# Gated attention mix on one core: a maxima product takes the PSUM bank whose last read stands first in VectorE's order, instead of a fixed turn of four

## The chip, the cores and the metric

The kernel runs on one core of a Trainium2 chip. The metric is the device time of one execution in microseconds (us); the number compared is the median of several runs. A profile is one execution taken by the hardware profiler; its span runs from the first to the last instruction.

The engines are named as the profile names them: PE is TensorE (PEld are its weight loads), DVE is VectorE, ACT is ScalarE, POOL is GpSimd, SP issues most DMAs. Each works through its own instructions in a fixed order and waits on semaphores for the others. Matmul results go to PSUM, which has eight banks of 128 x 512 float32 numbers here called by their tiles' names.

## What is computed

The input x has 2048 rows of 512 numbers. Two attentions of 32 heads of 16 numbers are formed on it and mixed by a gate:

```
q, k, v = x @ wqkv                                   # attention A, over all 2048 keys
o = softmax(q k^T * 0.25) v;  a = o @ wo
# attention B, in 4 segments of 512 rows, masked inside the segment:
p = softmax(q_s k_s^T * 0.25 + mask);  a_dot = p v_s
o = sig(beta) * a_mem + (1 - sig(beta)) * a_dot      # a_mem: memory of the earlier segments
b = o @ wo
g = sigmoid(sum(x * gate_w));  out = g * a + (1 - g) * b
```

Each softmax needs the largest score of each row before the exponentials, so that these cannot overflow.

## The kernel before

**Two stages.** In the first stage (up to about 300 us) the projections are computed and stored in DRAM. In the second, the work is cut into 64 units, 32 of side A and 32 of side B: a unit is four heads and one segment of 512 queries. A unit of A has 64 slots, a unit of B 10 slots, 2368 slots in all, and the second stage is one loop over slots, `n`.

**What one slot does.** `score_part(n)` (scores L744) multiplies keys by queries into a bank of the pool `st`, three banks in turn, and ScalarE takes the exponential into `p` (L767). `max_part(m)` works 96 slots ahead, `m = n + LEAD`: it forms scores of a later unit the other way round, queries by keys, in one of four fixed banks `sm0` to `sm3` (L205, called a maxima product here), and VectorE reduces the bank to row maxima. These are later put as extra rows beside that unit's queries, so that the score product subtracts them itself. After every third slot (`BURST` = 3) come the value products of older units, `ops` += v p (L801), or projections and output products that fill in. So TensorE's order in a burst is score, maxima, score, maxima, score, maxima, then values. The order of every engine is written out by the program; nothing is scheduled at run time.

**How VectorE reads a bank.** A product of side A fills a whole bank and is read by one TENSOR_REDUCE (L226). A product of side B has one or two pieces in the same bank, each read by a masked reduction (L238, in the profile CUSTOM_DVE_ANT_0 with a short DVE_READ_ACCUMULATOR2_ANT behind it). Only the first piece is read at once; the second goes into the list `rows_left` and is read after the next product's own reduction (`flush_rows`). So a two-piece B product m is read in the order: first piece of m, product m+1, second piece of m, product m+2. A unit of B has ten products, six of them in two pieces: 192 in all.

**Which bank.** In the second stage the call is

```python
            max_part(m, lambda: banks[m % 4])
```

Product m+4 writes where product m was, and waits until VectorE's last read of product m is done. In the first stage, where the first 96 products are made, another pool is used (`me_sm`), which the change leaves alone.

**The end.** The last maxima product is made at slot n = 2271. From slot 2274 on (`wide`) every other burst of scores goes to `sm1`, `sm2`, `sm3` by a fixed turn, and output products to `sm0` (L913).

Of the kernel before, what the change touches and what calls it, by code (L numbers as in the profile page):

```python
# [13 lines left out]
ALU = mybir.AluOpType  # L14
# [8 lines left out]
CH = 512  # L23
# [24 lines left out]
def gated_mix(ctx, tc, x, xT, wqkv, a_wo, b_wq, b_wk, b_wv, b_wo, beta, gate_w, out):  # L48
    nc = tc.nc
# [60 lines left out]
    nS = len(slots)  # L110
# [64 lines left out]
    tri = {}  # L175
# [3 lines left out]
    def finish_max(u):  # L179
        nm = pmt.pop(u)  # L180
        if u[0] == "A":
            pm, nm = nm, mp.tile([128, 4, 4], F32, tag="nm", name="nm")
            nc.vector.tensor_reduce(nm, pm, axis=AX.X, op=ALU.max, negate=True)  # L183

        ms = mp.tile([128, 2, 2, 2, 4], F32R, tag="ms", name="ms")
        nv = nm.rearrange("p (r h) s -> p r h s", r=2)
        nc.gpsimd.tensor_copy(ms[:, :, 0], nv)  # L187
        nc.gpsimd.tensor_sub(ms[:, :, 1], nv, ms[:, :, 0].bitcast(F32))
        return ms
# [14 lines left out]
    def max_product(ps, u, h, s, n0, n, k, k0=0):  # L204
        nc.tensor.matmul(ps[:, n0:n0 + n], rows(qt[u][:, :, s * 128:(s + 1) * 128], h, 48), rows(k[:, :, k0:k0 + n], h, 48),  # L205
                         start=True, stop=True)

    rows_left = []

    def flush_rows():  # L210
        while rows_left:
            rows_left.pop(0)()

    def max_part(m, bank):

        u, (r, i) = maxs[m]
        side, g, c = u
        if u not in pmt:
            pmt[u] = mp.tile([128, 4, 4] + [4] * (side == "A"), F32, tag="pm" + side, name="pm")
        pm = pmt[u]  # L220
        ps = bank()
        if side == "A":

            kc, s, h = i // 8, i % 8 // 2, 2 * r + i % 2
            max_product(ps, u, h, s, 0, CH, kt_[u, kc])
            nc.vector.tensor_reduce(pm[:, h, s, kc:kc + 1], ps, axis=AX.X, op=ALU.max)  # L226
            flush_rows()
        else:


            k = kt_[u, c]
            mine = [(2 * r + h, s, 128 * (s == 2) + 256 * (s == 1 and h), 128 * (s + 1))
                    for h, s in (((0, 0), (0, 2)), ((0, 1), (1, 1)), ((1, 0), (1, 2)), ((0, 3),), ((1, 3),))[i]]
            for h, s, n0, w in mine:
                max_product(ps, u, h, s, n0, w, k)
            flush_rows()
            for h, s, n0, w in mine:
                rows_left.append(lambda h=h, s=s, n0=n0, w=w: nc.vector.tensor_tensor_reduce(  # L238
                    out=tri["rest"][:, 0:w], in0=ps[:, n0:n0 + w], in1=tri["mask"][:, CH - w:], scale=-1.0, scalar=3.0e38,
                    op0=ALU.add, op1=ALU.min, accum_out=pm[:, h, s:s + 1]))  # L240
            rows_left.pop(0)()
        if m == last_max[u]:
            def finish():

                due = min(e for e in a_last if e >= last_max[u]) + LATE_T
                late.append((min(due, first[u] + LEAD - 12), u, finish_max(u)))
            todo.append((m + 1, finish))

    def run_todo(m):

        for e in [e for e in todo if e[0] <= m]:
            todo.remove(e)
            e[1]()

    def run_late(pool, tag, m):
        while us := [e for e in late if e[0] < m][:2]:
            for e in us:
                late.remove(e)
            transpose_max(us, pool, tag)
# [3 lines left out]
    def loads(m):  # L263

        m = min(m, len(maxs) - 1)
        while loaded[0] <= m:
            u, (r, i) = maxs[loaded[0]]
            if loaded[0] == first_max[u]:
                load_q(u)
            kc = u[2] if u[0] == "B" else i // 8  # L270
            if (u, kc) not in kt_:
                load_k(u, kc)
            loaded[0] += 1
# [3 lines left out]
    with ExitStack() as p0:  # L277
# [282 lines left out]
        def some_max():  # L560
            m = mnext[0]
            if m == LEAD:
                return
            loads(m + 3 + PRE)
            for i in range(4):
                max_part(m + i, lambda: me_sm.tile([128, CH], F32, tag="sm", name="sm"))
            run_todo(m + 3)
            mnext[0] += 4
            run_late(me_ps, "me", mnext[0])
# [54 lines left out]
    banks = [sm_ps.tile([128, CH], F32, name=f"sm{i}") for i in range(4)]  # L624
# [383 lines left out]
    def most():  # L1008

        if not queue:  # L1010
            return 0
        side = queue[0][1][0]
        left = SLOTS[side] - queue[0][2]
        over = 64 * (len(queue) - LOW) > (HIGH - LOW) * (left if side == "A" else 0)
        return ends[side].get(left, MOST + over)
# [3 lines left out]
    while n < nS or queue or beside or filled[0] < len(fill):  # L1019
        for f in beside.pop(n, []):  # L1020
            f()
        if n < nS:
            score_part(n)
        m = n + LEAD
        if m < nS:
            loads(m + PRE)

            max_part(m, lambda: banks[m % 4])
        run_todo(m)
        if n >= nS or n % (2 * BURST if n in wide else BURST) == (2 * BURST if n in wide else BURST) - 1:  # L1030
            taken = 0
            if shared:
                for _ in range(3):
                    shared.pop(0)()
            else:
                taken = some_values(n, 8 if n >= nS or n in wide else most())
            if n < 5:


                for i in range(4):  # L1040
                    nc.tensor.matmul(ops[:, 128 * i:128 * i + 128], identf, identf, start=True, stop=True)
            if any(e[0] < m + 1 for e in late):
                run_late(st_ps, "st", m + 1)
            else:

                for _ in range(0 if n >= nS and queue else 4 if n not in wide else 11 - taken if taken < 8 else 0):
                    if filled[0] == len(fill) or fill[filled[0]][0] > n:
                        break
                    fill[filled[0]][1]()
                    filled[0] += 1  # L1050
        n += 1
# [12 lines left out]
def build():  # L1064
    import concourse.bacc as bacc
    nc = bacc.Bacc("TRN2", target_bir_lowering=False, num_devices=1)
    shapes = {"x": (S, D), "xT": (D, S), "wqkv": (D, 3 * D), "a_wo": (D, D), "b_wq": (D, D), "b_wk": (D, D),
              "b_wv": (D, D), "b_wo": (D, D), "beta": (H,), "gate_w": (D,)}
    args = [nc.dram_tensor(n, s, F32, kind="ExternalInput").ap() for n, s in shapes.items()]
    out = nc.dram_tensor("out", (S, D), F32, kind="ExternalOutput").ap()  # L1070
    with tile.TileContext(nc) as tc:
        gated_mix(tc, *args, out)
    return nc
# [23 lines left out]
```

## Time and profile before

| | |
|---|---|
| median of 3 runs | 1779.55 us (1779.37 to 1779.65) |
| the profiled execution's own time | 1779.57 us |
| its span | 1777.8 us |
| POOL busy | 641.2 us |
| ACT, exponentials L767, x2261 | 1189.5 us busy, 601 ns each |
| DVE, reductions L226, x2048 | 1281.1 us busy, 683 ns each |
| DVE, masked reductions L238, x512 | 247.3 us busy, 483 ns each |
| PE, maxima products of A, L205, x2048 | 660.4 us busy, 428 ns each |
| PE, maxima products of B, L205, x512 | 166.2 us busy, 385 ns each |

An instruction's duration is longer than the time it takes up: two reductions in a row overlap by some 0.08 us at their ends, and matmuls overlap much more, so counts times durations come to more than the busy time. "Idle before" is the time in which an engine did nothing ahead of an instruction, with the instruction whose semaphore ended it. An engine can start late by less than the overlap and show no idle time.

### The profile page before, as it was taken

The numbers are of one execution on the slowest core, as the hardware profiler recorded it, in microseconds if no ns is written. First come the engines' busy times: TensorE is split into PE (matmuls) and PEld (weight loads), VectorE is DVE, ScalarE is ACT, GpSimd is POOL, SyncE is SP. The second block draws the span as 40 slices with busy tenths as digits, with TensorE's granted clock in tenths as the row PEclk, the third lists the DMA queues.
The fourth block names the chain that finished last, engine by engine and source line by source line (L and its number), as shares of the span: only waits on it lengthen the run. The fifth ranks groups of instructions, "written<-read, shape, count | busy, mean of one in ns | idle before, by whom it ended". The sixth has DMA issues, their size and how long they took to land.

```text
span 1777.8 us, 40673 instructions
## 1 busy us (share of the span) xinstructions
PE 1770.5 (100%) x14945; PEld 915.2 (51%) x14945; DVE 1573.5 (89%) x3331; ACT 1435.4 (81%) x2752; POOL 641.2 (36%) x748
## 2 busy tenths in 40 slices
PE   9999999999999999999999999999999999999999
PEld 8887776444444444444444444444444444444444
DVE  4236777999999999999999999999999999999931
ACT  5455445888888888888888888888888888888884
POOL 3002223415161417443434343344434253435343
PEclk9999999999999999999999999999999999999999
DMA  7667566445453536555454544454545353544542
GB/s 251 212 234 239 182 205 187 121 110 134 128 152 107 147 108 179 143 146 128 132 143 121 145 127 146 128 146 126 147 112 154 113 141 116 150 119 138 144 160 62
DMA packets 141270, 261.55 MB, mean 147 GB/s; under 512 B 36328, under 2 KB 58888, under 8 KB 140560
## 3 DMA queue, kind: packets, MB, share of 16 engines
q1 hardware_dynamic: 139712, 257.55, 50.3%
q8 instruction: 119, 1.95, 0.5%
q0 software_dynamic: 1216, 1.14, 0.3%
q14 instruction: 79, 0.65, 0.1%
q10 hardware_dynamic: 144, 0.26, 0.0%
HBM read 174.39 MB, written 83.25 MB: 145 GB/s over the span
## 4 chain that ended last, share of the span: by engine, by line
PE 95%; DVE 1%; ACT 1%; DMA 1%; POOL 1%; issue 0%; SPq 0%; POOLq 0%; DVEq 0%
PE ops L801 33%; PE st L744 27%; PE sm L205 14%; PE pr L311 10%; PE ops L913 4%; PE ops L684 2%; PE sm L913 2%; PE num L514 1%; POOL mn L378 1%; PE pr L401 1%; PE mps L545 0%; DVE pm L226 0%; DMA qdB<-q 0%; PE mt_ps L196 0%; DMA raw<-xT 0%; PE sm L744 0%
## 5 line engine op out<-in xcount | busy, mean ns | idle before, releaser
L767 ACT ACTIVATE p<-st 128x512 f32<-128x512 f32 x2261 | 1189.5, 601 | 152.3 <-PE sm L205 108.2
L226 DVE TENSOR_REDUCE pm<-sm 128x1 f32<-128x512 f32 x2048 | 1281.1, 683 | 11.5 <-PE sm L205 11.3
L744 PE MATMUL st<-qA,kA 50*128 50x512 f32 x2014 | 663.4, 432 | 0.0
L205 PE MATMUL sm<-kA,qA 48*128 48x512 f32 x2048 | 660.4, 428 | 0.4
L801 PE MATMUL ops<-p,vA 128*17 128x128 f32 (+3 forms) x6432 | 552.0, 442 | 0.0
L744 PEld LDWEIGHTS st<-qA,kA 50*128 50x128 f32 x2014 | 328.0, 185 | 415.1 <-ACT p L767 370.6
L205 PEld LDWEIGHTS sm<-kA,qA 48*128 48x128 f32 x2048 | 331.7, 185 | 16.9 <-issue 4.6
L863 POOL TENSOR_TENSOR rcp<-rec,minus 128x32 f32<-128x32 f32 x43 | 234.2, 5446 | 76.4 <-DMA rec<-dend 71.8
L238 DVE CUSTOM_DVE_ANT_0 rest<-sm,mask 128x128 f32<-128x128 f32 (+3 forms) x512 | 247.3, 483 | 1.4
L801 PEld LDWEIGHTS ops<-p,vA 128*17 128x17 f32 x6432 | 130.5, 96 | 214.4 <-issue 189.4
L748 POOL TENSOR_SCALAR_AFFINE_SELECT p<-p 128x512 f32<-128x512 f32 x128 | 79.4, 636 | 324.9 <-ACT p L767 320.4
L205 PE MATMUL sm<-kB,qB 48*128 48x128 f32 (+3 forms) x512 | 166.2, 385 | 0.0
L744 PE MATMUL st<-qB,kB 50*128 50x512 f32 (+1 forms) x495 | 109.3, 330 | 0.3 <-ACT mt L199 0.3
L381 DVE TENSOR_TENSOR q<-full,q 128x512 fp32r<-128x512 f32 x56 | 38.6, 689 | 74.9 <-ACT q L374 67.9
L744 PEld LDWEIGHTS st<-qB,kB 50*128 50x128 f32 x495 | 69.9, 186 | 59.3 <-ACT p L767 48.6
L801 PE MATMUL ops<-p,vB 128*17 128x128 f32 (+3 forms) x1504 | 87.5, 350 | 0.0
L205 PEld LDWEIGHTS sm<-kB,qB 48*128 48x128 f32 x512 | 80.0, 184 | 0.0
L187 POOL CAST ms<-nm 128x16 fp32r<-128x16 f32 x32 | 6.3, 196 | 201.5 <-DVE nm L183 199.6
L378 POOL TENSOR_SCALAR mn<-full 128x512 f32<-128x512 f32 x24 | 36.4, 1515 | 102.5 <-ACT full L373 82.2
L373 ACT COPY full<-pr 128x512 f32<-128x512 f32 x56 | 32.8, 586 | 40.2 <-PE pr L311 37.3
L187 POOL CAST ms<-pm 128x16 fp32r<-128x16 f32 x32 | 6.3, 196 | 127.9 <-DVE pm L238 127.8
L801 PEld LDWEIGHTS ops<-p,vB 128*17 128x17 f32 x1504 | 33.1, 97 | 31.1 <-issue 26.6
(198 smaller groups left out, 1622.7 us busy)
## 6 DMA issues: line engine op xcount, KB each, us to landing
kA<-kdA SPq DMA_DIRECT2D x256, 128.0 KB
vA<-vdA SPq DMA_DIRECT2D x31, 544.0 KB
kA<-kdA SPq DMA_DIRECT2D x256, 64.0 KB
kdA<-q SPq DMA_DIRECT2D x32, 256.0 KB
qdB<-q SPq DMA_DIRECT2D x32, 256.0 KB
qA<-qdA SPq DMA_DIRECT2D x64, 128.0 KB
kdB<-q SPq DMA_DIRECT2D x32, 256.0 KB
qB<-qdB SPq DMA_DIRECT2D x64, 128.0 KB
```

What stands on the lines that cost most here:

```text
L205: nc.tensor.matmul(ps[:, n0:n0 + n], rows(qt[u][:, :, s * 128:(s + 1) * 128], h, 48), rows(k[:, :, k0:k0 + n], h, 48), start=True, stop=True)
L226: nc.vector.tensor_reduce(pm[:, h, s, kc:kc + 1], ps, axis=AX.X, op=ALU.max)
L238: rows_left.append(lambda h=h, s=s, n0=n0, w=w: nc.vector.tensor_tensor_reduce(out=tri["rest"][:, 0:w], in0=ps[:, n0:n0 + w], in1=tri["mas ...
L311: nc.tensor.matmul(ps, l(a, k), r(b, k), start=(n == 0), stop=(n == 11))
L378: nc.gpsimd.tensor_scalar_min(ph["mn"], full, 0.0)
L381: nc.vector.tensor_sub(q2, full, q1.bitcast(F32))
L744: nc.tensor.matmul(ps[:, n0:n0 + CH - q0], rows(k[:, :, b * 128:(b + 1) * 128], h, 50), rows(q[:, :, q0:], h, 50), start=True, stop=True)
L748: nc.gpsimd.affine_select(out=x, in_=x, pattern=[[0, 4], [1, 128]], base=0, channel_multiplier=-1, compare_op=ALU.is_ge, fill=0.0)
L767: nc.scalar.activation(p[:, h], ps, AF.Exp, scale=SCALE)
L801: nc.tensor.matmul(ops[32 * h:32 * h + 17, q0:q0 + 128 * w], v[:, 17 * h:17 * h + 17], p[:, h, c0:c0 + 128 * w], start=(i == 0), stop=done ...
L863: eng.tensor_tensor(r, rec, minus, op=ALU.pow)
L913: yield lambda i=i, x=x, w=w: nc.tensor.matmul(ps, t[:, b, x], halved[side][:, o, w], start=start and i == 0, stop=stop and i == 2)
```

## The change

The program now keeps, for each of the four banks, the place in VectorE's order of the bank's last read (`read_last`), and gives each maxima product of the second stage the bank with the earliest such place. The count goes up by one with each reduction that is issued. No instruction is added on VectorE or TensorE, and none changes its place: only the bank that each one names changes, and with it the semaphore value that a product waits for.

```diff
+    read_last = dict(zip(range(4), range(4)))
+
+    def oldest():
+
+        return min(read_last, key=read_last.get)
+
+    def was_read(b):
+
+        if b is not None:
+            read_last[b] = count[0] = count[0] + 1
+    count = [4]
+
-    def max_part(m, bank):
+    def max_part(m, bank, b=None):
...
             nc.vector.tensor_reduce(pm[:, h, s, kc:kc + 1], ps, axis=AX.X, op=ALU.max)
+            was_read(b)
             flush_rows()
         else:
...
             k = kt_[u, c]
+            if b is not None:
+                read_last[b] = 9 * nS
...
+            def masked(h, s, n0, w):
+                nc.vector.tensor_tensor_reduce(
+                    out=tri["rest"][:, 0:w], in0=ps[:, n0:n0 + w], in1=tri["mask"][:, CH - w:], scale=-1.0, scalar=3.0e38,
+                    op0=ALU.add, op1=ALU.min, accum_out=pm[:, h, s:s + 1])
+                was_read(b)
+
             for h, s, n0, w in mine:
-                rows_left.append(lambda h=h, s=s, n0=n0, w=w: nc.vector.tensor_tensor_reduce(
-                    out=tri["rest"][:, 0:w], in0=ps[:, n0:n0 + w], in1=tri["mask"][:, CH - w:], scale=-1.0, scalar=3.0e38,
-                    op0=ALU.add, op1=ALU.min, accum_out=pm[:, h, s:s + 1]))
+                rows_left.append(lambda h=h, s=s, n0=n0, w=w: masked(h, s, n0, w))
             rows_left.pop(0)()
...
-            max_part(m, lambda: banks[m % 4])
+            b = oldest()
+            max_part(m, lambda: banks[b], b)
```

The change adds lines, so that L226 of the kernel before is L238 now, L238 is L253, L744 is L763, L801 is L820; L205 keeps its number.

VectorE, around products 307 to 311 (at about 433 us of the profile). `ISA rest` is a masked reduction, the short `ISA pm` belongs to it; `sm0` to `sm3` are the banks (the number behind the underscore is the tile's own). Before:

```order
L226 TENSOR_REDUCE pm_4661<-sm3_3011 128x1
L238 ISA rest_3023,pm_4743<-sm2_3010,mask_3024 128x256
L238 ISA pm_4743 128x1
L226 TENSOR_REDUCE pm_4661<-sm0_3008 128x1
L238 ISA rest_3023,pm_4743<-sm1_3009,mask_3024 128x256
L238 ISA pm_4743 128x1
L226 TENSOR_REDUCE pm_4661<-sm2_3010 128x1
```

The rows are: product 307, second piece of 306, product 308, first piece of 309, product 310. Product 310 reads from `sm2`, the bank of 306, whose second piece was read after product 307.

The same rows now:

```order
L238 TENSOR_REDUCE pm_4661<-sm0_3008 128x1
L253 ISA rest_3023,pm_4743<-sm3_3011,mask_3024 128x256
L253 ISA pm_4743 128x1
L238 TENSOR_REDUCE pm_4661<-sm2_3010 128x1
L253 ISA rest_3023,pm_4743<-sm1_3009,mask_3024 128x256
L253 ISA pm_4743 128x1
L238 TENSOR_REDUCE pm_4661<-sm0_3008 128x1
```

Product 310 now reads from `sm0`, the bank of 307, whose only read stands one place earlier than the second piece of 306.

TensorE at the same place, with the engines that each row waits for: the burst of products 309, 310, 311 (sm) with its scores (st) and the first value products (ops) behind it. Before:

```order
L205 MATMUL sm1_3009<-kB1_201,qB30_4543 128x256 [waits DVE_49]
L205 MATMUL sm1_3009<-kB1_201,qB30_4543 128x256
L744 MATMUL st_4873<-qB20_3911,kB0_200 128x512 [waits Activation_49]
L205 MATMUL sm2_3010<-kA1_193,qA40_4466 128x512 [waits DVE_49]
L744 MATMUL st_4879<-qB20_3911,kB0_200 128x512 [waits Activation_49]
L205 MATMUL sm3_3011<-kA1_193,qA40_4466 128x512
L801 MATMUL ops_3012<-p_4820,vA_4043 17x512 x4
```

The fourth row, product 310, waits for the second piece of 306; product 311 needs the bank of 307, which was read before that, so it carries no wait of its own.

The same rows now:

```order
L205 MATMUL sm1_3009<-kB1_201,qB30_4543 128x256 [waits DVE_49]
L205 MATMUL sm1_3009<-kB1_201,qB30_4543 128x256
L763 MATMUL st_4873<-qB20_3911,kB0_200 128x512 [waits Activation_49]
L205 MATMUL sm0_3008<-kA1_193,qA40_4466 128x512 [waits DVE_49]
L763 MATMUL st_4879<-qB20_3911,kB0_200 128x512 [waits Activation_49]
L205 MATMUL sm3_3011<-kA1_193,qA40_4466 128x512 [waits DVE_49]
L820 MATMUL ops_3012<-p_4820,vA_4043 17x512 x4
```

Product 310 waits for the read of 307, and product 311, one pair later, for the second piece of 306. The two waits have changed places, and 311 carries one now. Over the program 2354 maxima products carry a wait for VectorE, before it was 2162: 192 more, one for each B product in two pieces. The instructions on TensorE that do nothing but wait are 697 in both.

At the end of the second stage the last four products, which stood in `sm0`, `sm1`, `sm2`, `sm3`, stand in `sm2`, `sm3`, `sm0`, `sm1`.

## The prediction

> **What bounds the kernel now.** I read the page first, then the busy time by stretches, then the chain of waits, then the waits of the maxima products alone, and last the order in time around one such wait. From the page:
>
> ```profile
> span 1777.8 us, 40673 instructions
> PE 1770.5 (100%) x14945; PEld 915.2 (51%) x14945; DVE 1573.5 (89%) x3331; ACT 1435.4 (81%) x2752; POOL 641.2 (36%) x748
> PE 95%; DVE 1%; ACT 1%; DMA 1%; POOL 1%; issue 0%; SPq 0%; POOLq 0%; DVEq 0%
> ```
>
> VectorE's 89% is a mean over stages. By stretches (length, then busy time of PE, PEld, DVE, ACT and POOL, the clock, the DMA share and GB/s) two engines are full in the stage that the change touches:
>
> ```profile
> 0.00:260.00 260.00, 257.19 (x1180) 201.54 (x1180) 135.28 (x245) 131.06 (x228) 47.56 (x59) 1.00 0.66 221
> 500.00:700.00 200.00, 199.99 (x1917) 92.25 (x1917) 199.73 (x423) 176.69 (x343) 82.80 (x98) 1.00 0.50 135
> 1300.00:1500.00 200.00, 200.00 (x1862) 93.19 (x1856) 199.75 (x428) 177.80 (x345) 82.72 (x92) 1.00 0.48 131
> ```
>
> In the second stage VectorE works 199.7 us of 200 and TensorE 200 of 200, at full clock. They run at one pace. The chain of waits goes over TensorE for 95% of the span, yet VectorE has nearly nothing to give either, and the change takes no work from it. What can be gained is then only time in which TensorE stands still for a bank while VectorE is also late, before or after. So the first number to look for is how long maxima products wait for a bank. The waits of the weight loads from 304 to 1702 us, where the products of the second stage lie (total us, times, longest):
>
> ```profile
> PEld st L744 <- ACT p L767: 411.7, 795, 0.9
> PEld sm L205 <- DVE pm L238: 4.0, 13, 0.5
> PEld sm L205 <- DVE pm L226: 0.4, 2, 0.3
> ```
>
> L238 is the masked reduction. Product m+4 waits for the last read of product m, and where m is a B product in two pieces that read is an L238. The large first row is no fault of the banks: weight loads take a fraction of the matmuls' time, and they stand idle while matmuls run. The matching view of VectorE, by groups in the same stretch, with the idle time at the end of the row:
>
> ```profile
> L226 DVE TENSOR_REDUCE pm<-sm 128x1 f32<-128x512 f32 x1952 | 1221.5, 683 | 0.3
> L238 DVE CUSTOM_DVE_ANT_0 rest<-sm,mask 128x512 f32<-128x512 f32 x128 | 87.6, 684 | 0.0
> ```
>
> VectorE practically never stands idle for a product. Whatever the banks cost TensorE, VectorE has seen 0.3 us of it as open idle time.
>
> **The change part by part.** Nothing is added to any engine; 192 products swap the wait with their successor, and 192 more products carry a wait. I take the gain first, then the price of the waits, then the end of the stage.
>
> *The wait that moves.* One of the 13 waits of the row above, in order of time (start, length, engine, line):
>
> ```profile
> 433.53 0.68 DVE L226 TENSOR_REDUCE pm<-sm 128x1 f32<-128x512 f32 x1
> 433.85 0.50 PE L205 MATMUL sm<-kB,qB 48*128 48x256 f32 x2
> 434.13 0.41 DVE L238 CUSTOM_DVE_ANT_0 rest<-sm,mask 128x256 f32<-128x256 f32 x1
> 434.61 0.19 PEld L205 LDWEIGHTS sm<-kA,qA 48*128 48x128 f32 x2 [0.34 <-DVE pm L238]
> 434.61 0.50 PE L205 MATMUL sm<-kA,qA 48*128 48x512 f32 x2
> 434.95 0.39 PE L744 MATMUL st<-qB,kB 50*128 50x512 f32 x1
> 435.07 0.41 DVE L238 CUSTOM_DVE_ANT_0 rest<-sm,mask 128x256 f32<-128x256 f32 x1
> 435.26 1.05 PE L801 MATMUL ops<-p,vA 128*17 128x512 f32 x8
> 436.36 1.28 DVE L226 TENSOR_REDUCE pm<-sm 128x1 f32<-128x512 f32 x2
> ```
>
> The second piece of 306 is read from 434.13 to 434.54, and product 310 starts at 434.61. Its successor 311 follows at once (the same row counts 2), the third score at 434.95 and the values at 435.26. With the change, 310 waits only for the reduction that ends at 433.53 + 0.68 = 434.21, and could start some 0.3 us sooner; 311 now waits for the second piece and starts at 434.61, as before. The third score slips between the two. Values start 435.26 - 434.95 = 0.31 us after the burst's last matmul; that matmul would be 311 at 434.61 in place of the score at 434.95, so the values come up to 0.34 us sooner. Elsewhere nothing is won: 192 products are in question and 13 of them show an idle wait. All 13 sum to 4.0 us, the upper end of the gain.
>
> *What of it reaches the end.* VectorE is not waiting for product 310 in that stretch. It reads the next masked piece from 435.07, and reductions run on at 436.36. An earlier product shortens the program only where VectorE is late itself. That happens, hidden in the overlap of its instructions:
>
> ```profile
> 467.07 3.07 DVE L226 TENSOR_REDUCE pm<-sm 128x1 f32<-128x512 f32 x5
> 470.23 0.29 DVE L238 CUSTOM_DVE_ANT_0 rest<-sm,mask 128x128 f32<-128x128 f32 x1
> ```
>
> Five reductions take 3.07 us and the last is 0.68 long, so one starts every (3.07 - 0.68) / 4 = 0.60 us; the sixth instruction was due at 467.07 + 5 x 0.60 = 470.06 or so and started at 470.23, 0.17 us late. If each of the 13 waits bought back one such lateness, the gain would be 13 x 0.17 = 2.2 us; if VectorE is never late before the next full set of banks takes the lead away again, it is 0. The lead cannot be kept: four banks are all there are, and a product that comes sooner waits sooner. The stretch above is nearer to the low end, because 1.8 us after the wait VectorE is still fed. I take 0.5 us, an estimate between 0 and 2.2.
>
> *Where the trace and a rule part.* The Trainium skill (Perfetto Trace Analysis, Optimization Strategy) says to find the gaps on the engine that is most contended, name the semaphore that ends them, and make that dependency come sooner. Taken for TensorE this would credit the whole row, 4.0 us, and stands as a rival below. The trace does not bear it out in full, since VectorE is as full as TensorE: 199.7 of 200 us.
>
> *The waits that are added.* A pair of rows prices them. Product 1109 carries a wait for VectorE and product 1112 carries none; both are the third of a burst that begins with a B product in two pieces:
>
> ```profile
> 925.73 0.40 PE L205 MATMUL sm<-kA,qA 48*128 48x512 f32 x1
> 926.02 0.40 PE L205 MATMUL sm<-kA,qA 48*128 48x512 f32 x1
> 927.88 0.39 PE L205 MATMUL sm<-kA,qA 48*128 48x512 f32 x1
> 928.17 0.39 PE L205 MATMUL sm<-kA,qA 48*128 48x512 f32 x1
> ```
>
> 926.02 - 925.73 = 0.29 us with the wait, 928.17 - 927.88 = 0.29 us without. So a wait that is already met costs nothing that these rows can show, to 0.01 us: at most 192 x 0.01 = 1.9 us. The other end is a wait that is an instruction of its own on TensorE's queue:
>
> ```profile
> L205 PEldq EVENT_SEMAPHORE  x447: 51/51/51, 160.0 to 1688.0; - x149
> ```
>
> 192 x 0.051 = 9.8 us. The new waits stand in the matmul's own row, and the instructions that only wait are 697 in both programs, so I take 0. Should a moved wait bind, the third product is behind it, then the values, then the next burst's first score and with it ScalarE; but the time at which the third product may start is the time at which the second one started before.
>
> *The end of the stage.* The scores that follow in `sm1` to `sm3`, and the output products in `sm0`, take the banks by a fixed turn, and two of these banks are now read last by a later reduction:
>
> ```profile
> 1700.74 1.88 DVE L226 TENSOR_REDUCE pm<-sm 128x1 f32<-128x512 f32 x3
> 1703.74 0.62 PE L744 MATMUL sm<-qA,kA 50*128 50x512 f32 x3
> 1705.06 0.96 PE L913 MATMUL sm<-wA,blk 128*128 128x512 f32 x3
> ```
>
> The last reduction ends at 1702.62, and the first score on these banks starts at 1703.74, 1.12 us later, whichever bank it takes. The cover is the value products and scores in between; were it gone, the price would be two reductions, 1.2 us. I take 0.
>
> *The sum.* 1779.57 us for the profiled execution (span 1777.8 and 1.8 around it), less 0.5, plus 0, plus 0: 1779.1 us, span 1777.3. The median of the runs shown is 1779.55, 0.02 below the profiled one, so 1779.1 stands for the median too.
>
> **The rivals.** *The whole bank wait comes back.* TensorE is the one bound, and each of its 4.0 us is a microsecond: 1779.57 - 4.0 = 1775.6. For it speaks the chain with PE at 95%; against it VectorE's 0.3 us of idle time: it would have to go faster than it is shown to go. This is the case by the Trainium skill's rule above. Chance 0.11.
>
> *The added waits cost.* Slower: TensorE's sequencer takes time over each of the 192 new waits, in the third product of a burst, right ahead of the values, on an engine that has no idle time. At the full 51 ns it is 1779.57 + 9.8 = 1789.4; it decides once a wait costs more than 3.56 / 192 = 19 ns. For it speaks that PE is busy 200 of 200 us; against it the equal 0.29 us. Chance 0.09.
>
> *The change does not do what it says.* The rows of the change show the swap in place, and the record of a bank is right although the mark for a read still to come is overwritten by the first piece's read: at the next product that bank is the youngest in any case. I give this nothing of its own; it would read as no change.
>
> **How the numbers follow.** What a measurement of this kernel can tell from no change is about 0.2%, 3.56 us. The likeliest case, little or nothing comes back, has 0.80 and lies within it. Faster by more needs nearly the whole row of 4.0 us, 0.11; slower by more needs 19 ns for each added wait, 0.09. The range: at the fast end the 2.2 us of the lateness bound give 1777.4, and I go to 1776.8 to take in part of the first rival; at the slow end 1.9 us of waits that the rows cannot resolve on top of 1779.1 give 1781.0.
>
> **What would show it.** Right: the row of maxima products waiting for the masked reduction falls from 4.0 us to well below 1, nothing new of that size appears for L205, VectorE stays at 199.7 of 200 us, the third score of such a burst starts ahead of its third product, and the span is within 1 us of 1777.8. The first rival would show VectorE's reductions closer together and the second stage ending some 4 us sooner than 1702.6. The second would show third products more than 0.29 us behind the second ones where no bank is awaited. I am wrong if VectorE's busy share falls in the second stage, or if scores after 1703 us wait for a reduction.

## The result: 3.5 us faster, and the profile after

| | before | changed |
|---|---|---|
| median | 1779.65 us (1779.0 to 1781.19, 13 runs) | 1776.16 us (1774.71 to 1776.89, 13 runs) |
| profiled execution | 1779.57 us | 1776.47 us |
| span | 1777.8 us | 1774.8 us |

The ratio is 0.9978 with a 95% interval of 0.9970 to 0.9986. The gain is near the 4.0 us of the row of bank waits, more nearly than the waits of that row account for, as the experiments show. From the page of the changed kernel:

```profile
span 1774.8 us, 40674 instructions
PE 1767.2 (100%) x14945; PEld 917.1 (52%) x14945; DVE 1570.2 (88%) x3331; ACT 1435.2 (81%) x2752; POOL 641.1 (36%) x748
PE 96%; DMA 1%; ACT 1%; DVE 1%; POOL 1%; issue 0%; SPq 0%; POOLq 0%; ACTq 0%
```

The same number of matmuls and reductions is done, yet PE and DVE are each busy 3.3 us less (1770.5 and 1573.5 before): the gain was inside time that counts as busy. By stretches in the second stage (same columns as before) nothing can be seen, since both engines are still full:

```profile
500.00:700.00 200.00, 200.00 (x1923) 92.59 (x1919) 199.80 (x424) 177.23 (x343) 83.13 (x98) 1.00 0.49 135
1300.00:1500.00 200.00, 200.00 (x1869) 93.35 (x1871) 199.80 (x427) 178.18 (x346) 82.72 (x92) 1.00 0.49 133
```

The waits of the weight loads for maxima products, 304 to 1702 us (total us, times, longest):

```profile
PEld sm L205 <- DVE pm L238: 0.7, 3, 0.3
PEld sm L205 <- DVE pm L253: 0.5, 3, 0.2
```

Together 1.2 us, against 4.0 + 0.4 = 4.4 before: 3.2 us of listed waits went, and 3.5 us of time. At the place that the prediction showed, the order in time is now:

```profile
434.31 0.50 PE L205 MATMUL sm<-kB,qB 48*128 48x256 f32 x2
434.55 0.42 DVE L253 CUSTOM_DVE_ANT_0 rest<-sm,mask 128x256 f32<-128x256 f32 x1
434.69 0.18 PEld L205 LDWEIGHTS sm<-kA,qA 48*128 48x128 f32 x1
435.00 0.18 PEld L763 LDWEIGHTS st<-qB,kB 50*128 50x128 f32 x1
435.03 0.18 PEld L205 LDWEIGHTS sm<-kA,qA 48*128 48x128 f32 x1
435.03 0.46 PE L763 MATMUL st<-qB,kB 50*128 50x512 f32 x1
435.45 1.05 PE L820 MATMUL ops<-p,vA 128*17 128x512 f32 x8
```

Product 310 starts at 434.69 with no idle time ahead of it, 434.69 - 434.31 = 0.38 us after the burst's B product (434.61 - 433.85 = 0.76 before). Product 311 and the third score start together at 435.03, the score's weights a little ahead (435.00). The values start 435.45 - 434.31 = 1.14 us after the B product, 435.26 - 433.85 = 1.41 before: 0.27 us sooner.

### The profile page after: what moved, and what is told of

The parts are those of the page before. It is cut to its first block, busy times and chain, and to the rows that moved or that the text cites. A ratio compares the mean times of both kernels' runs of the same rounds, so it can differ in the third digit from the quotient of the medians.

```text
span 1774.8 us, 40674 instructions
## 1 busy us (share of the span) xinstructions
PE 1767.2 (100%) x14945; PEld 917.1 (52%) x14945; DVE 1570.2 (88%) x3331; ACT 1435.2 (81%) x2752; POOL 641.1 (36%) x748
## 3 DMA queue, kind: packets, MB, share of 16 engines
q0 software_dynamic: 1216, 1.14, 0.3%
## 4 chain that ended last, share of the span: by engine, by line
PE 96%; DMA 1%; ACT 1%; DVE 1%; POOL 1%; issue 0%; SPq 0%; POOLq 0%; ACTq 0%
PE ops L820 33%; PE st L763 27%; PE sm L205 14%; PE pr L330 10%; PE ops L932 4%; PE ops L703 2%; PE sm L932 2%; PE num L533 1%; POOL mn L397 1%; PE pr L420 1%; PE mps L564 0%; DMA qdB<-q 0%; PE mt_ps L196 0%; DMA raw<-xT 0%; PE sm L763 0%; DVE jk L492 0%
## 5 line engine op out<-in xcount | busy, mean ns | idle before, releaser
L238 DVE TENSOR_REDUCE pm<-sm 128x1 f32<-128x512 f32 x2048 | 1282.3, 688 | 11.3 <-PE sm L205 11.2
L205 PE MATMUL sm<-kA,qA 48*128 48x512 f32 x2048 | 670.4, 427 | 0.2
L763 PE MATMUL st<-qA,kA 50*128 50x512 f32 x2014 | 659.0, 432 | 0.0
L820 PE MATMUL ops<-p,vA 128*17 128x128 f32 (+3 forms) x6432 | 552.7, 441 | 0.0
L763 PEld LDWEIGHTS st<-qA,kA 50*128 50x128 f32 x2014 | 326.8, 185 | 421.2 <-ACT p L786 372.9
L205 PEld LDWEIGHTS sm<-kA,qA 48*128 48x128 f32 x2048 | 337.9, 185 | 12.7 <-issue 4.2
L253 DVE CUSTOM_DVE_ANT_0 rest<-sm,mask 128x128 f32<-128x128 f32 (+3 forms) x512 | 249.3, 487 | 1.3
L820 PEld LDWEIGHTS ops<-p,vA 128*17 128x17 f32 x6432 | 130.8, 96 | 208.6 <-issue 184.0
L205 PE MATMUL sm<-kB,qB 48*128 48x128 f32 (+3 forms) x512 | 166.1, 384 | 0.0
L763 PE MATMUL st<-qB,kB 50*128 50x512 f32 (+1 forms) x495 | 107.7, 331 | 0.3 <-ACT mt L199 0.3
L763 PEld LDWEIGHTS st<-qB,kB 50*128 50x128 f32 x495 | 68.5, 186 | 60.8 <-ACT p L786 48.7
L820 PE MATMUL ops<-p,vB 128*17 128x128 f32 (+3 forms) x1504 | 87.5, 350 | 0.0
L205 PEld LDWEIGHTS sm<-kB,qB 48*128 48x128 f32 x512 | 79.9, 184 | 0.0
L898 POOL TENSOR_TENSOR v<-v,inv 128x512 f32<-128x512 f32 x31 | 39.9, 1287 | 24.1 <-DMA inv<-rdA 20.6
```

What stands on the lines that cost most here:

```text
L253: nc.vector.tensor_tensor_reduce(out=tri["rest"][:, 0:w], in0=ps[:, n0:n0 + w], in1=tri["mask"][:, CH - w:], scale=-1.0, scalar=3.0e38, op ...
L763: nc.tensor.matmul(ps[:, n0:n0 + CH - q0], rows(k[:, :, b * 128:(b + 1) * 128], h, 50), rows(q[:, :, q0:], h, 50), start=True, stop=True)
L820: nc.tensor.matmul(ops[32 * h:32 * h + 17, q0:q0 + 128 * w], v[:, 17 * h:17 * h + 17], p[:, h, c0:c0 + 128 * w], start=(i == 0), stop=done ...
L898: eng.tensor_mul(k["v"], k["v"], k["inv"])
```

## The experiments

After the result two theories stood against each other, and a third that had to be put aside. *A: the lead is kept.* TensorE comes to the values sooner, stays ahead for many products, and VectorE is late less often, in amounts that its overlap hides. *B: shorter reductions.* Other banks, or another execution, make VectorE's instructions themselves a little quicker. *C: chance.* Any program built anew would differ as much, whatever its banks.

### Controls: nothing changed, and the change once more

`null` is the kernel before with the call written otherwise; `after_again` is the changed kernel with its table written otherwise.

```diff
-            max_part(m, lambda: banks[m % 4])
+            max_part(m, lambda: banks[(m + 0) % 4])
```

> The kernel before, unchanged, as a second profile of it and a measure of the noise. Both theories: ratio 1.000 within 0.001, 1779.6 us. Theory A (bank waits come back): the row of maxima products waiting for the masked reduction is 4.0 us again. Theory B (each reduction became shorter by about 1 ns because of the banks it reads): the reductions of side A start 598 ns apart as in the first profile. If this profile has them 597 ns apart, B is only the difference of two executions.

```diff
-    read_last = dict(zip(range(4), range(4)))
+    read_last = {n: n for n in range(4)}
```

> The changed kernel, unchanged, for a second profile and on the same chip as the others: 1776.2 within 1, and A's reductions 598 ns apart again where its first profile had 597; if they are 597 again, about 0.7 ns x 1947 = 1.3 us of the gain is not explained by waits.

`null`: 1779.73 us, ratio 1.0001 (0.9992 to 1.0010). `after_again`: 1776.47 us, ratio 0.9980 (0.9971 to 0.9989). C falls. In the first profile of the changed kernel a reduction of A lasted 688 ns in the mean; in the second it lasted 683, as before, at the same time to 0.3 us. From start to start of two such reductions in a row there are 598 ns (median) in the kernel before, in `null` and in `after_again`, and 597.5 in the first profile of the change. The group of the A reductions in `after_again`, 304 to 1702 us:

```profile
L238 DVE TENSOR_REDUCE pm<-sm 128x1 f32<-128x512 f32 x1952 | 1220.3, 683 | 0.1
```

So B falls too: the gain is there whether these rows read 688 or 683, and with the same distance between reductions. And the waits for a bank in `null`, then in `after_again`:

```profile
PEld sm L205 <- DVE pm L238: 3.9, 13, 0.5
PEld sm L205 <- DVE pm L226: 0.4, 2, 0.3
```

```profile
PEld sm L205 <- DVE pm L238: 0.7, 3, 0.3
PEld sm L205 <- DVE pm L253: 0.7, 4, 0.2
```

### The change in two halves

The six two-piece products of a unit are of three kinds: index 0 and 2 (128 and 384 wide) and index 1 (256 and 256). In each half only some second pieces count as a bank's last read; for the others the first piece counts, as the fixed turn would have it.

```diff
-                was_read(b)
+                if (h, s) == mine[0][:2] or i in (1,):
+                    was_read(b)
```

> The change for the B products with index 1 alone (two pieces of 256; they have 9 of the 13 long waits, 0.3 us each); the others are counted as if read at once, which is the fixed turn. Theory A: 9 x 0.33 = 3.0 us of the 4.0 come back, 1776.7. Theory B: the banks of all products move on from the first swap, so the whole gain, 1776.2. If the short waits of the other 128 products matter: 1778 or more.

> The complement: the change for the B products with index 0 and 2 alone. Theory A: the waits of 0.3 us stay, at most 1.0 us comes back, 1778.6. Theory B: 1776.2.

`only_1`: 1777.45 us, ratio 0.9989 (0.9981 to 0.9998), 2.3 us below `null`. `only_0_2` (the same with `(0, 2)`): 1778.83 us, ratio 0.9995 (0.9986 to 1.0003), 0.9 below `null`, which its interval alone does not tell from nothing. The sum, 3.2, agrees with the 3.5 of the change to within what the runs tell apart. The waits of `only_1`, then of `only_0_2`:

```profile
PEld sm L205 <- DVE pm L253: 1.2, 4, 0.5
PEld sm L205 <- DVE pm L238: 0.4, 2, 0.3
```

```profile
PEld sm L205 <- DVE pm L253: 3.5, 12, 0.3
PEld sm L205 <- DVE pm L238: 0.7, 3, 0.3
```

In `only_1` 4.3 - 1.6 = 2.7 us of listed waits went, and 2.3 us of time, less than the 3.0 that its expectation took from the long waits. In `only_0_2` the listed waits hardly fall, from 4.3 to 4.2, though the time fell by some 0.9.

Where VectorE gains is seen when its starts are sorted. For each read of a bank I took the time since the start of the read before it, grouped the reads by their place in the unit (slots since the unit's first B product; a unit here runs from there to the next unit's first B product), and summed each place over the units. The places with the largest difference to `null`, in us:

```
place in the unit   change   only_1   only_0_2
18                   -0.87             -0.92
25                   -1.03    -1.02
48                   -0.48    -0.38
54                   -0.47    -0.36
```

An empty cell means that the half does not recover that place. The two-piece products of index 1 stand at the places 12 and 15; the product that takes the bank of the first of them is at 16, as 310 is. Taking the waits there away brings VectorE forward at 25, 48 and 54, that is 9 to 38 products later. Those of index 0 and 2 stand at 0, 3, 24 and 27, and what they give shows at 18. The products right behind a wait are not among these places.

The list of waits leaves out most of the waits behind this, because it names only idle times above 0.15 us. The bank itself tells more: product 310, which waits, starts 0.06 us after the last read of its bank has ended. I compared every product's start with that end in 28 units, all with B products but the first two and the last. In `null` 38 products stand at this distance, 19 at place 7 and 19 at place 16, at least one in each unit. The list has nine of them, 2.8 us, all at place 16 of every third unit; most of what else it has lies in the first unit with B products and stays in the change. In the changed kernel no product waits at place 7 and nine at place 16. The other 18 that stand near this distance are third products of a burst, which start 1.4 us or more ahead of their read. In `only_1` the 19 at place 7 still wait and nine at 16, and 29 at 28 and 31 are new; in `only_0_2` none waits at 7, and 28 wait at 16. So each half frees the place whose gain it shows, and `only_0_2` gains from waits that the list does not name.

It also follows that listed waits and time do not go one for one. The nine units with such a wait took 1.2 us less in all (`after_again`: 1.1) for the 2.8 us of waits that went there. Of the 3.6 us between `null` and the change 2.2 were won in units without a listed wait. That the sums of the two, 3.2 and 3.5 us, are so near is luck.

The lead can be seen as well. In those nine units the product at place 18 starts 0.70 us ahead of its read in `null` and 0.93 us in the changed kernel. Of these 0.23 us more, 0.16 are left at place 25, 0.07 at 39 and nothing at 48. At 25 and at 48 the lead falls by about what VectorE gains there (0.05 to 0.06 us in each unit); the rest is lost without such a gain. This is theory A, and one such place can be followed in the rows. After the wait at 434.61 of the kernel before, VectorE is fed for six microseconds; then, behind a short piece (128 wide, 0.28 us), product 319 is late. VectorE in the kernel before, then in the changed one:

```profile
440.55 0.28 DVE L238 CUSTOM_DVE_ANT_0 rest<-sm,mask 128x128 f32<-128x128 f32 x1
440.75 0.08 DVE L238 DVE_READ_ACCUMULATOR2_ANT pm<- 128x1 f32 x1
440.80 0.69 DVE L226 TENSOR_REDUCE pm<-sm 128x1 f32<-128x512 f32 x1
```

```profile
440.96 0.28 DVE L253 CUSTOM_DVE_ANT_0 rest<-sm,mask 128x128 f32<-128x128 f32 x1
441.17 0.09 DVE L253 DVE_READ_ACCUMULATOR2_ANT pm<- 128x1 f32 x1
441.17 0.69 DVE L238 TENSOR_REDUCE pm<-sm 128x1 f32<-128x512 f32 x1
```

In the changed kernel the reduction starts with the accumulator's row (441.17 and 441.17); before, it starts 0.05 us behind it (440.75, 440.80), without a gap that the idle column would show. A larger one, five reductions at places 17 to 21 of a later unit, which has no listed wait but one of the 19 at place 7, before and changed:

```profile
1437.22 3.20 DVE L226 TENSOR_REDUCE pm<-sm 128x1 f32<-128x512 f32 x5
```

```profile
1434.95 3.09 DVE L238 TENSOR_REDUCE pm<-sm 128x1 f32<-128x512 f32 x5
```

The same five take 0.11 us less, and the second row starts 2.27 us sooner.

### Reading both pieces at once, with the fixed turn

If the wait is the cause, the fixed turn is as good as the new rule once no read of a bank is put off. Here the second piece is read right behind the first; nothing else differs from the kernel before.

```diff
-            rows_left.pop(0)()
+            flush_rows()
```

> The fixed turn of banks, but the second piece of a B product is read right behind the first, so that no product waits for a late second read: the same release of banks as in the change, reached without the choice of banks. Theory A: the gain of the change, 1776 us, waits for the masked reduction under 1 us. Theory B: the banks are the old turn, so no gain from the reductions, 1778 us or more. My forecast's theory (a lead that is lost again): 1779.1.

1795.35 us, ratio 1.0086 (1.0073 to 1.0100): far from the 1776 that was expected. VectorE in `at_once`, at the first such pair of a unit:

```profile
436.59 0.42 DVE L238 CUSTOM_DVE_ANT_0 rest<-sm,mask 128x256 f32<-128x256 f32 x1
436.93 0.09 DVE L238 DVE_READ_ACCUMULATOR2_ANT pm<- 128x1 f32 x1
437.05 0.42 DVE L238 CUSTOM_DVE_ANT_0 rest<-sm,mask 128x256 f32<-128x256 f32 x1
```

The second piece starts 0.46 us after the first and not at 436.93, with the accumulator's row. In the trace it carries a wait for a semaphore that VectorE sets itself, and it starts when that row has ended (436.93 + 0.09 = 437.02). Both write the same columns of the scratch tile `rest`. The next run gives them the columns that they read, which never meet within one product.

```diff
-                    out=tri["rest"][:, 0:w], in0=ps[:, n0:n0 + w], ...
+                    out=tri["rest"][:, n0:n0 + w], in0=ps[:, n0:n0 + w], ...
...
-            rows_left.pop(0)()
+            flush_rows()
```

> As the run with the second piece read at once, but the two masked reductions write separate columns of the scratch tile, so the second no longer waits for the first to end. In the run before this one the second started 0.46 us after the first, where 0.34 us is usual: 0.12 us x 192 = 23 us, against the 15.6 us lost. If that wait is the loss, and theory A holds (bank waits come back once no product waits for a late second read), this gives the change's time with the fixed turn of banks: 1776. If two masked reductions in a row cost by themselves, it stays near 1795. If the choice of banks does something beyond the waits, it comes to 1779.

1775.80 us, ratio 0.9975 (0.9966 to 0.9985). VectorE there, and the waits for a bank:

```profile
434.21 0.42 DVE L238 CUSTOM_DVE_ANT_0 rest<-sm,mask 128x256 f32<-128x256 f32 x1
434.55 0.09 DVE L238 DVE_READ_ACCUMULATOR2_ANT pm<- 128x1 f32 x1
434.55 0.42 DVE L238 CUSTOM_DVE_ANT_0 rest<-sm,mask 128x256 f32<-128x256 f32 x1
```

```profile
PEld sm L205 <- DVE pm L226: 1.5, 8, 0.3
```

The pair now stands 0.34 us apart, and the second piece of this pair carries no wait. The pairs of 128 and 384 columns gain as much (0.33 us apart, then 0.21). 0.12 us for each of 192 pairs is 23 us; between the two runs lie 1795.35 - 1775.80 = 19.6 us. With that out of the way the fixed turn gives the gain of the change, by another road: no product at place 7 or 16 waits for its bank, the listed waits are as low (1.5 us), and the time is the same. The order of banks is worth nothing in itself; what counts is how long a product waits for one.

### Putting the second piece off by one product more

This makes the wait larger. The second piece is read after two further products in place of one, with the fixed turn and with the new rule.

```diff
-
-    def flush_rows():
-        while rows_left:
+    rows_at = [0]
+
+    def flush_rows(m=None):
+        while rows_left and (m is None or m >= rows_at[0] + 2):
             rows_left.pop(0)()
...
-            flush_rows()
+            flush_rows(m)
...
             rows_left.pop(0)()
+            rows_at[0] = m
```

> The kernel before with the second piece read one product later still, fixed turn: the wait made larger, to see its rate of exchange. Each of the 192 products is released one reduction (0.60 us) later. Theory A: about 0.45 us of wait on each, 86 us in the waits' rows, of which the third product of the burst catches up some 0.25 us each: 1779.6 + 192 x 0.2 = about 1818. My forecast's theory (TensorE's lead is lost or regained on its own, so waits hardly reach the end): under 1785.

> The same later read with the change's choice of banks. Worked out from the two orders, every product then again has at least three reductions between the release of its bank and its own, as in the change. Theory A: the change's time, 1776 within 1.5, whatever the fixed turn loses. If the choice of banks does not act by the distance of the release: as slow as the fixed turn.

`defer2_turn`: 1863.51 us, ratio 1.0469 (1.0455 to 1.0483). `defer2_oldest`: 1797.62 us, ratio 1.0103 (1.0088 to 1.0118). Both are far above what was expected, 1818 and 1776. With the fixed turn, only one read now stands in VectorE's order between the second piece and the product that takes its bank. The waits for a bank of `defer2_turn`, 304 to 1790 us:

```profile
PEld sm L205 <- DVE pm L239: 76.2, 173, 0.9
```

76.2 + 0.4 us of waits (the rest for plain reductions) in place of 4.4 is 72 more; the time rose by 1863.51 - 1779.95 = 83.6. The other 11 us may be the idle time ahead of the masked reductions, which `defer2_oldest` has too (304 to 1702 us, last column); with the fixed turn this was not tried.

```profile
L254 DVE CUSTOM_DVE_ANT_0 rest<-sm,mask 128x128 f32<-128x128 f32 x498 | 241.1, 484 | 15.2
```

Put off by two, the second piece of one product falls right before the first piece of the next, and the scratch tile binds as in `at_once`. Apart, as there:

> The later second read with the change's choice of banks, and the two masked reductions in separate columns of the scratch tile. Where the later read puts a second piece right ahead of the next B product's first, the two then no longer wait for each other. If that wait (15.2 us of idle time ahead of the masked reductions, 1.4 in the changed kernel) was the 21 us that run lost, and the choice of banks does what the distances say, this comes to 1776 to 1779. If the later read costs through the banks in spite of the distances, it stays above 1790.

1780.56 us, ratio 1.0000 (0.9992 to 1.0009): 17 us of the excess were the scratch tile's, and the idle time ahead of the masked reductions is 2.2 us. The 1776 to 1779 us that were expected were not reached. Its waits:

```profile
PEld sm L205 <- DVE pm L239: 4.3, 20, 0.3
```

The list stands where it stood in the kernel before, and so does the time. By ratio it is 0.0025, 4.4 us, above `at_once_apart`, for 2.8 us more of listed waits. The order of reads differs too, and the list leaves out short waits, so this is no price of a wait; what keeps this run from the change's time stays open.

### Other places for the products and the pieces

Three runs looked for what is left, on top of the change. In two, B products stand second or third in a burst in place of first; in one, the wide piece of index 0 and 2 is read first and the narrow one put off.

```diff
-        at_ = [next(m for m in range(len(maxs) + start, len(maxs) + start + 6) if m % 3 == 0)]
+        at_ = [next(m for m in range(len(maxs) + start, len(maxs) + start + 6) if m % 3 == 1)]
```

This is `place_1`; in `place_2` the range begins at `len(maxs) + start - 1` and the test is `m % 3 == 2`.

> The changed kernel with every B product in the second place of its burst instead of the first. Of the lateness that VectorE still has, most lies where a burst's first product is a B product in two pieces (0.70 us from its matmul to its read, against 0.57 for A). Second and third products come 0.3 to 0.7 us ahead of need. If lateness at the first product is what is left to win, 2 to 4 us: 1773. If VectorE's lateness only moves to the burst behind, 1776.

> The same with every B product in the third place, where products come about 1.3 us ahead of their read. Same expectation: 1772 to 1774 if first products were what is left, 1776 if the lateness only moves.

```diff
-                    for h, s in (((0, 0), (0, 2)), ((0, 1), (1, 1)), ((1, 0), (1, 2)), ((0, 3),), ((1, 3),))[i]]
+                    for h, s in (((0, 2), (0, 0)), ((0, 1), (1, 1)), ((1, 2), (1, 0)), ((0, 3),), ((1, 3),))[i]]
```

> The changed kernel with the wider piece of the B products of index 0 and 2 first (384 columns ahead of 128, products and reads alike). A first read of 0.47 us in place of 0.21 lets the next product come 0.26 us later without VectorE being late. If lateness right behind short first reads is part of what is left, 0.5 to 1.5 us less than the changed kernel, 1775; if the lateness only moves on, 1776.3. A difference under 1 us will show in the profile's spacing more than in the median.

`place_1`: 1782.18 us, ratio 1.0010 (1.0001 to 1.0019). `place_2`: 1794.55 us, ratio 1.0079 (1.0065 to 1.0093). The first two were expected between 1772 and 1776 and came out slower than the kernel before. `wide_first`: 1776.02 us, ratio 0.9978 (0.9969 to 0.9987), no different from the change, which fits its second expectation, that the lateness only moves on. `place_2` is the one that teaches. Its waits for a bank, then VectorE's reductions, 304 to 1702 us:

```profile
PEld sm L205 <- DVE pm L238: 0.9, 5, 0.3
```

```profile
L238 DVE TENSOR_REDUCE pm<-sm 128x1 f32<-128x512 f32 x1934 | 1208.1, 683 | 19.2 <-PE sm L205 14.4 <-PE st L763 2.7
```

The listed waits are as low as in the change, and VectorE now stands idle for 19.2 us, 14.4 of them for a maxima product, and all but 0.1 right behind a masked reduction. From a burst's last product to the next burst's first lie 1.1 to 1.4 us on TensorE, filled by values; within a burst most products lie 0.24 to 0.34 us apart. With the B product last, its first piece alone (0.21 to 0.47 us of VectorE's time) stands ahead of that long gap. So short bank waits are not enough: what VectorE has to read at the burst's end counts as well. That this is the whole cause was not tried by itself.

## Why the prediction was wrong, point by point

**The wait that moves: right but for one sign.** Product 310 came without idle time ahead of it, 311 started when it had started before, 0.73 us after the B product (0.76), and the values came 0.27 us sooner, forecast as up to 0.34. The larger part of the row fell from 4.0 to 0.5 us, forecast as well below 1. The third score was to start ahead of 311 and started together with it.

**What of it reaches the end: this step failed.** It took 0.5 us, between 0 and 2.2; measured are 3.5. Four things in it were wrong.

- "Elsewhere nothing is won": it counted the 13 waits of the list and no other. In each of the 28 units at least one product waited for its bank, 38 in all, and 2.2 us of the gain came in units without a listed wait.
- "The lead cannot be kept: four banks are all there are, and a product that comes sooner waits sooner." The leads are kept over 9 to 38 products, until VectorE is late.
- "1.8 us after the wait VectorE is still fed" was a look at the wrong place. It is fed, and late six microseconds on, at product 319. The wait and the time that it costs stand far apart, which is no sign that the one does not cause the other.
- The size of a lateness, 0.17 us, came from a stretch that the bank waits do not touch. The same place in the changed kernel:

```profile
467.39 3.08 DVE L238 TENSOR_REDUCE pm<-sm 128x1 f32<-128x512 f32 x5
470.56 0.29 DVE L253 CUSTOM_DVE_ANT_0 rest<-sm,mask 128x128 f32<-128x128 f32 x1
```

470.56 - 467.39 = 3.17 us, 470.23 - 467.07 = 3.16 before: this lateness stays. The upper bound, 13 x 0.17 = 2.2 us, was built on it. In place of 13 latenesses of 0.17 us the runs show about 0.12 us in each of nearly 30 units, in pieces of 0.05 to 0.1 us.

**The first rival** came nearest in its number: 1775.6 forecast, 1776.16 measured. Against it stood VectorE's 0.3 us of idle time, "it would have to go faster than it is shown to go". It did: two reads overlap by some 0.08 us, and a read that is late by less shows no idle time. From the start of its first read in the second stage to the start of its last VectorE took 1397.6 us before and 1393.9 after: 3.7 us less, of which the row of the A reductions shows 0.2 as idle time (0.3 and 0.1). But "each of its 4.0 us is a microsecond" is not what happened: the nine waits of 2.8 us gave back 1.2, and waits outside the row gave the rest. Its number is luck.

The Trainium skill (Perfetto Trace Analysis, Optimization Strategy) says to find the gaps on the engine in question and to make what ends them come sooner. Here that points at the right dependency; that the whole row, 4.0 us, comes within 0.5 us of the gain is the same luck.

**The added waits: right, as far as the runs show.** 192 more products carry a wait. The second rival's 9.8 us would have made the change slower, and third products would have stood more than 0.29 us behind the second ones. At place 29, where none waits for its bank, the mean is 0.29 us in the kernel before and in the changed one, and `at_once_apart`, with the fixed turn, comes to the same time as the change (ratios 0.9975 and 0.9978).

**The end of the stage: right.** The last reduction ends at 1697.66 + 1.88 = 1699.54, and the first score on these banks starts 1.12 us later, as before:

```profile
1697.66 1.88 DVE L238 TENSOR_REDUCE pm<-sm 128x1 f32<-128x512 f32 x3
1700.66 0.63 PE L763 MATMUL sm<-qA,kA 50*128 50x512 f32 x3
```

The stage itself ends 1702.62 - 1699.54 = 3.08 us sooner, which is the difference of the two spans, 3.0: all of the gain is made inside it. (It began 0.6 us later in this profile, so the gain from its first read to its last is the 3.7 us above.)

## What to carry to other kernels

Where two full engines hand work to each other through few buffers, do not count only the waits that a list of idle times names: compare each product's start with the end of the last read of its buffer. Then look for the engine that pays many products later, in start-to-start distances and not in the idle column. The listed waits gave no price here: 2.8 us of them were worth 1.2. Before changing which buffer is taken, count for each product how many reads lie between the buffer's last read and its own: reading the late piece earlier did as much here as choosing another bank. And give instructions that stand side by side different scratch, even when nobody reads it.

## What the runs showed of the hardware

Two masked reductions with an accumulator, back to back and writing the same scratch columns, start 0.46 us apart, and 0.34 us apart when they write different ones (256 wide). With the same columns the second carried a semaphore wait and started once the first's accumulator row had ended (437.02 and 437.05 us in `at_once`). The scratch is never read; over 192 pairs it cost 19.6 us, over five times what the change brings.

A product that waited for its bank started 0.06 us after the masked reduction that last read it had ended (the 38 products of `null`).
